# A windowed-attention and gated-feed-forward block: later chunks' normalized rows turned through DRAM and 32x32 blocks

## The chip, the core and the metric

The kernel runs on one core of one Trainium2 chip. The metric is device time in microseconds, median of the runs. One core has TensorE (matrix products; its weight loads are shown as a stream of their own), VectorE, ScalarE, GpSimd and SyncE (SP), which issues most DMA transfers. Each engine works off its own list of instructions in order; semaphores hold an instruction back until what it reads is there. A DMA issue waits on its queue too, so what stands behind a waiting issue waits with it.

## The reference

The block takes 2048 rows of 640 features, all inputs bf16. It normalizes the rows, computes attention over a sliding window of 256 rows with 32 heads of 20, and a gated feed-forward with 1536 hidden features, and adds both to the input.

```python
def reference(A_x, A_wqkv, A_wo, B_x, B_w_gate, B_w_up, B_w_down):
    x = A_x
    xn = _layernorm(x, axis=-1)          # (x - mean) / sqrt(var + 1e-5)
    return x + _A_ref(xn, A_wqkv, A_wo) + _B_ref(xn, B_w_gate, B_w_up, B_w_down)

def _A_ref(x, wqkv, wo):
    B, S, D = x.shape
    H = 32; Dh = D // H; W = 256
    qkv = (x @ wqkv).reshape(B, S, 3, H, Dh).transpose(2, 0, 3, 1, 4)
    q, k, v = qkv[0], qkv[1], qkv[2]
    scores = jnp.einsum("bhqd,bhkd->bhqk", q, k) * (Dh ** -0.5)
    idx = jnp.arange(S)
    mask = (idx[:, None] - idx[None, :] >= 0) & (idx[:, None] - idx[None, :] < W)
    p = _softmax(jnp.where(mask[None, None], scores, -1e9), axis=-1)
    o = jnp.einsum("bhqk,bhkd->bhqd", p, v)
    return o.transpose(0, 2, 1, 3).reshape(B, S, D) @ wo

def _B_ref(x, w_gate, w_up, w_down):
    g = jnp.einsum("bsd,df->bsf", x, w_gate)
    u = jnp.einsum("bsd,df->bsf", x, w_up)
    return jnp.einsum("bsf,fd->bsd", _sigmoid(g) * u, w_down)
```

## The kernel before

**Chunks.** The rows go in four chunks of 512 (c = 0 to 3), each of four blocks of 128 rows (s). A chunk's rows lie in xc, rows on partitions. They are normalized into xn, and turned into xnT, features on partitions: 5 groups (d) of 128 features by 512 rows. All projections read xnT, one group after the other as five accumulating matmuls.

**Stages of a chunk.** g_qk makes Q and K in five blocks each; VectorE (Q) and ScalarE (K) copy each block out of PSUM to st, and SP sends it to a scratch in DRAM and reads it back spread over heads (spread). g_v makes V: per row block two halves, copied out by VectorE (first half) and ScalarE. g_gu makes the twelve blocks (f) of the feed-forward: a gate product pg with a tanh on ScalarE, an up product pu, and h from both on VectorE. scores, and pv later, run the attention in groups of heads: products into ps, an exponential on ScalarE into pT, masks on pT by GpSimd (the affine selects), products into acc; finish_group and scale_group transpose and scale acc on VectorE into oc. g_out makes the output: per row block the down projection over the twelve h (down), the wo product (add_wo), the addition of x (add_x) and the store.

**The order.** It is written out by hand, as a list of parts (fill) that the attention steps pull work from: an attention step's products go to TensorE, and then as much of the other work as its credit allows. All g_... functions are generators that emit a piece of work and yield its cost on TensorE. mix(a, b, first, every, rest) emits a piece of b behind every `every`-th piece of a from piece `first` on, and with rest what is left of b at the end. Pieces of cost 0 (VectorE's, DMA issues) change nothing in TensorE's order. Each engine's list follows the order of emission; the accumulators come from four PSUM banks in turn (ps_d), so a product waits until the bank's reader from four products ago is done.

**The norms.** Chunk 0's are made in the prologue and turned by TensorE (transpose_rows). For chunks 1 to 3, g_norms emits per row block the statistics (ln_block, two BN_STATS and an aggregation; behind the fourth, GpSimd makes rstds of all four), then `gap` empty pieces, then per block the norm (norm_block, L272), and a piece later that block's transfer from xn to xnT, a transposing DMA on SP (turn_block, L283). xn has four buffers of 128 x 640. Chunk 3's transfers are emitted apart (g_turns). Where they stand:

- norms1 (chunk 1): behind the feed-forward pieces of chunk 0 (gu0a from its fifth piece, gu0b);
- norms2: in out0, chunk 0's output part;
- norms3: statistics behind gu1b's pieces (chunk 1's feed-forward blocks 7 to 11), norms and transfers in out1, with the gap of 6.

**SP's list around chunk 1.** load_rest (L187) issues the last four quarters of the feed-forward weights, then spread of chunk 0's other head groups; then come chunk 1's four transfers, chunk 2's rows (load_x), wo by way of a DRAM tile (turn_wo), wd, and the zero rows of the second scratch. The last quarter, wu[1] from FS // 2 on, holds up-weights for the blocks f = 9 to 11. SP has eight completion semaphores in turn, so an issue also waits for the landing of the one eight before it.

**Others that the change touches.** make_edge (L238) fills the tile edge for masks of later chunks, on GpSimd, after chunk 0's g_qk; new_rows (L447) loads x's rows for the last addition into the three rows buffers and, for the last block, into an xn buffer.

Of the kernel before, what the change touches and what calls it, by code (L numbers as in the profile page):

```python
# [9 lines left out]
P = 128  # L10
S = 2048
D = 640
# [3 lines left out]
DC = D // P  # L16
FC = F // P
CW = 512
NCH = S // CW
SBC = CW // P  # L20
# [6 lines left out]
FS = 768  # L27
# [4 lines left out]
MULT = mybir.AluOpType.mult  # L32
SUB = mybir.AluOpType.subtract
# [60 lines left out]
def kernel(  # L94
# [85 lines left out]
    def load_gu(t, w, k, lo=0, hi=FS):  # L180
        nc.sync.dma_start(out=t[k][:, :, lo:hi],
                          in_=w.rearrange("(c p) f -> p c f", p=P)[:, :, k * FS + lo:k * FS + hi])
# [7 lines left out]
    def load_rest():  # L190
        load_gu(wg, B_w_gate, 1, 0, FS // 2)
        load_gu(wu, B_w_up, 1, 0, FS // 2)
        load_gu(wg, B_w_gate, 1, FS // 2)
        load_gu(wu, B_w_up, 1, FS // 2)
        spread("q", 0, 4, NG)
        spread("k", 0, 4, NG)

# [38 lines left out]
    edge = const.tile([P, HG, 2 * U], BF16, name="edge")  # L236

    def make_edge():  # L238
        nc.gpsimd.memset(edge, BIG)
        for k, base, sign in ((0, -1, -1), (1, 0, 1)):  # L240
            for a in range(2):
                view = edge[a * U:(a + 1) * U, :, k * U:(k + 1) * U]
                nc.gpsimd.affine_select(out=view, in_=view, pattern=[[0, HG], [sign, U]],
                                        compare_op=GE, fill=0.0, base=base, channel_multiplier=-sign)

    xnT = {}
    xns = {}

    def ln_half(c, s, a, stats=None):
        if a == 0:  # L250
# [17 lines left out]
        return rstds  # L268

    def norm_block(c, s, mv, rstd):  # L270
        xn = lnp.tile([P, D], BF16, name="xn")
        nc.vector.tensor_scalar(out=xn, in0=xc[c][:, s, :], scalar1=mv[:, 0:1],  # L272
                                scalar2=rstd[:, 0:1], op0=SUB, op1=MULT)
        xns[c, s] = xn

    def transpose_rows(s, copy, lo=0, hi=DC):
        pt = ps_h.tile([P, DC, P], BF16, name="pt", tag="h")
        for d in range(lo, hi):
            nc.tensor.transpose(pt[:, d, :], xns[0, s][:, d * P:(d + 1) * P], ident)  # L279
        copy(out=xnT[0][:, lo:hi, s * P:(s + 1) * P], in_=pt[:, lo:hi, :])  # L280

    def turn_block(c, s):
        nc.sync.dma_start(out=xnT[c][:, :, s * P:(s + 1) * P], in_=xns.pop((c, s)), transpose=True)  # L283

    def new_xnT(c):
        xnT[c] = xtp.tile([P, DC, CW], BF16, name="xnT")
# [53 lines left out]

    MM = 216

    def g_norms(c, turn, gap=3):


        new_xnT(c)
        mvs = lnp.tile([P, SBC, nc.vector.BN_AGGR_DIM], FP32, name="mvs", bufs=1)
        for s in range(SBC):
            ln_block(c, s, mvs[:, s, :])
            if s == SBC - 1:  # L350
                rstds = rstd_blocks(mvs)
            yield 0
        for _ in range(gap):
            yield 0
        for s in range(SBC):
            norm_block(c, s, mvs[:, s, :], rstds[:, s:s + 1])
            yield 0
            if turn:
                turn_block(c, s)

    def g_turns(c):
        for s in range(SBC):
            turn_block(c, s)
            yield 0

    def g_qk(c):
        for w in "qk":
            for m in range(DC):
                proj_block(w, c, m)
                if c == 0 and w == "q" and m == 1:  # L370
                    load_x(1)
                if c == 0 and w == "q" and m == 3:
                    load_gu(wu, B_w_up, 0, FS // 2)
                if c == 1 and w == "q" and m == 3:
                    load_wo()
                if c and w == "k" and m == DC - 1:
                    spread("q", c, 0, GH)
                yield 5 * MM
        if c == 0:
            spread("q", c, 0, 2)  # L380
            spread("k", c, 0, 2)
            spread("q", c, 2, 4)
            spread("k", c, 2, 4)
# [60 lines left out]
            out=rows[:, cut[0]:cut[1]], in0=y[:, 0:cut[1] - cut[0]], scalar=0.5,  # L444
            in1=rows[:, cut[0]:cut[1]], op0=MULT, op1=ADD)

    def new_rows(c, s, name="rows", bufs=3, queue=nc.sync):  # L447
        rows = lnp.tile([P, D], BF16, name=name, bufs=bufs)
        queue.dma_start(out=rows, in_=xr[:, c * SBC + s, :])
        return rows  # L450

# [11 lines left out]
    def g_out(c, between, ahead=()):  # L463
        nxt = new_rows(c, 0)
        for s in range(SBC):
            rows = nxt
            if s == 0:
                yield from ahead
            if s + 1 < SBC:
                nxt = new_rows(c, s + 1)  # L470
            ys = [ps_d.tile([P, CW], FP32, name=f"y{i}", tag="d") for i in range(2)]
            for y, cut in zip(ys, HALVES):
                yield from down(c, s, y, cut)
            if s == 0:
                yield from between
            outp(c, s, ys, rows)
            yield 10 * 136
# [117 lines left out]
    def mix(a, b, first, every=1, rest=True):  # L595

        for k, cost in enumerate(a):
            yield cost
            if k >= first and (k - first) % every == 0:
                yield next(b, 0)  # L600
        if rest:
            yield from b
# [9 lines left out]
        norm_block(0, s, mv, r)  # L612

    def mean_act(s):
        xn = lnp.tile([P, D], BF16, name="xn")
        neg = lnp.tile([P, 1], FP32, name="neg")
        nc.scalar.activation(out=xn, in_=xc[0][:, s, :], func=IDENTITY, scale=-1.0 / D, accum_out=neg)  # L617
        return xn, neg
# [7 lines left out]
    def norm_act(s, xn, neg, r):  # L626
        nc.vector.reciprocal(r, r)
        nc.vector.tensor_scalar(out=xn, in0=xc[0][:, s, :], scalar1=neg[:, 0:1],  # L628
                                scalar2=r[:, 0:1], op0=ADD, op1=MULT)
        xns[0, s] = xn  # L630

    new_xnT(0)
    for s in range(SBC):
        new_v(0, s)
    act, dve = nc.scalar.copy, nc.vector.tensor_copy
# [33 lines left out]
    nc.scalar.activation(out=scr, in_=neghalf[:, 0:1], func=EXP)  # L669
    banks.close()  # L670
    ps_s = banks.enter_context(tc.tile_pool(name="ps_s", bufs=1, space=bass.MemoryType.PSUM))
    for _ in g_qk(0):
        pass
    load_rest()
    make_edge()

    fill = Fill()
    GU = 10 * MM
# [4 lines left out]
        load(*args)  # L683
        yield 0

    norms1 = g_norms(1, True)
    norms2 = g_norms(2, True)
    norms3 = g_norms(3, False, 6)
    fill.add("gu0a", mix(g_gu(0, 0, 4), norms1, 4, 1, False), 4 * GU)
    fill.add("gu0b", mix(g_gu(0, 4, 12), norms1, 0), 8 * GU)  # L690
    fill.add("x2", later(load_x, 2), 0)
    fill.add("wo_i", later(turn_wo), 0)
    fill.add("wd", later(load_wd), 0)
    fill.add("pads", later(clear_next), 0)
    fill.add("qk1", g_qk(1), 50 * MM)
    fill.add("v1", mix(g_v(1), g_gu(1, 0, 2), 1, 2), 40 * 136 + 2 * GU)
    fill.add("out0", mix(g_out(0, g_gu(1, 2, 3)), norms2, 1, 1), OUT + GU)
    fill.add("x3", later(load_x, 3), 0)
    fill.add("qk2", g_qk(2), 50 * MM)
    fill.add("v2", mix(g_v(2), g_gu(1, 3, 7), 0, 1), 40 * 136 + 4 * GU)  # L700
    fill.add("gu1b", mix(g_gu(1, 7, 12), norms3, 0, 1, False), 5 * GU)
    fill.add("out1", mix(g_out(1, g_gu(2, 0, 1)), itertools.chain(norms3, g_turns(3)), 1, 2), OUT + GU)
    fill.add("qk3", g_qk(3), 50 * MM)
    fill.add("v3", mix(g_v(3), g_gu(2, 1, 5), 0, 1), 40 * 136 + 4 * GU)
    fill.add("gu2", g_gu(2, 5, 12), 7 * GU)
# [41 lines left out]
        for _ in gen:  # L747
            pass

    homes = [("rows", 3)] * (SBC - 1) + [("xn", 4)]  # L750
    rows = [new_rows(c, s, *home, queue=nc.scalar) for s, home in enumerate(homes)]
    banks.close()
    ps_y = pool("ps_y", 4, space=bass.MemoryType.PSUM)
    ys = {}
# [52 lines left out]
```

## Time and profile before

| what | value |
|---|---|
| median of 3 runs | 309.23 us (308.93 to 309.33) |
| span of the profiled execution | 307.5 us |
| TensorE busy in it | 299.6 us |
| VectorE busy | 170.7 us |
| ScalarE busy | 198.4 us |
| GpSimd busy | 169.3 us |
| chunk 1's transposing transfers issued | 39.32 to 44.59 us |
| chunk 2's | 93.28 to 101.35 us |
| chunk 3's | 162.58 to 173.89 us |

The span goes from the first to the last instruction of the program; the runs' time has launch and end around it, 1.7 us. In an order of time each row shows start, duration, engine, line, operation, tiles, count, and in brackets the idle time before it with what ended it. Where two instructions of one engine overlap by some ten ns, the later has begun before the earlier has drained; the distance of their starts is what one of them costs the engine. A row of a group has busy time and the mean of one in ns. A row of a stretch has its limits, its length, each engine's busy time and count in the order TensorE, its weight loads, VectorE, ScalarE, GpSimd, and then TensorE's granted clock, the DMA engines' share and GB/s.

### The profile page before, as it was taken

How to read it: one execution, taken by the hardware profiler on the slowest of the kernel's cores; microseconds unless marked ns; L12 is line 12 of the kernel's file. 1: busy time of each engine (PE TensorE's matmuls, PEld its weight loads, DVE VectorE, ACT ScalarE, POOL GpSimd, SP SyncE). 2: the span in 40 equal slices, each digit the busy share in tenths (PEclk: the TensorE clock that was granted, in tenths of full speed). 3: DMA queues.
4: the chain of work that ended last, by engine and by line, in shares of the span. 5: the costliest groups of instructions: out<-in, count | busy, mean ns of one | idle time of the engine just before them, and what ended most of it. 6: DMA issues, size and time to landing. Idle time of an engine off the chain costs nothing.

```text
span 307.5 us, 9944 instructions
## 1 busy us (share of the span) xinstructions
PE 299.6 (97%) x4276; PEld 167.5 (54%) x4311; DVE 170.7 (56%) x339; ACT 198.4 (65%) x197; POOL 169.3 (55%) x308
## 2 busy tenths in 40 slices
PE   7999999999999999999999999999999999999995
PEld 3654444555657654554457654554546664444774
DVE  5633666639698364487946164392824536363523
ACT  6933877698855649888674547878585547687000
POOL 6000686787874828576683729467372937566000
PEclk9999999999999999999999999999999999999999
DMA  7997976986407352820002712730000200000202
GB/s 215 366 344 236 324 158 214 337 238 209 154 2 139 58 179 68 272 83 2 3 3 67 129 58 87 250 122 0 5 0 2 87 26 21 2 2 7 83 21 67
DMA packets 40460, 35.68 MB, mean 116 GB/s; under 512 B 10560, under 2 KB 39872, under 8 KB 40384
## 3 DMA queue, kind: packets, MB, share of 16 engines
q1 hardware_dynamic: 39552, 34.27, 37.3%
q10 hardware_dynamic: 864, 0.77, 0.9%
q8 instruction: 34, 0.56, 0.8%
q14 instruction: 10, 0.08, 0.1%
HBM read 23.63 MB, written 10.26 MB: 110 GB/s over the span
## 4 chain that ended last, share of the span: by engine, by line
PE 96%; issue 1%; DMA 1%; DVE 1%; ACT 0%; SPq 0%
PE y L432 18%; PE pu L418 17%; PE pg L411 17%; PE pqk L297 14%; PE ps L487 9%; PE pv L326 7%; PE y L439 7%; PE acc L520 6%; DMA xc<-in_A_x_dram 1%; PE pt L279 0%; ACT xn L617 0%; DVE xn L272 0%; DVE xn L628 0%; SPq L156 0%; DVE stats L252 0%
## 5 line engine op out<-in xcount | busy, mean ns | idle before, releaser
L504 POOL TENSOR_SCALAR_AFFINE_SELECT pT<-pT 64x512 bf16<-64x512 bf16 (+1 forms) x256 | 157.7, 616 | 108.1 <-ACT pT L493 95.6
L493 ACT ACTIVATE pT<-ps 128x2048 bf16<-128x2048 f32 (+1 forms) x76 | 141.0, 1855 | 59.6 <-PE ps L487 54.6
L422 DVE SCALAR_TENSOR_TENSOR h<-th,pu 128x512 bf16<-128x512 f32 x48 | 32.8, 684 | 52.6 <-PE pu L418 46.1
L418 PE MATMUL pu<-xnT,wu 128*128 128x512 bf16 x228 | 59.0, 380 | 0.7 <-issue 0.2
L411 PE MATMUL pg<-xnT,wg 128*128 128x512 bf16 x226 | 58.5, 380 | 0.9 <-issue 0.3
L432 PE MATMUL y<-wd,h 128*128 128x320 bf16 (+2 forms) x396 | 56.7, 295 | 0.0
L432 PEld LDWEIGHTS <-h 128*128 128x128 bf16 x396 | 36.7, 98 | 15.8 <-issue 2.0
L414 ACT ACTIVATE th<-pg 128x512 f32<-128x512 f32 x48 | 28.6, 595 | 15.5 <-PE pg L411 15.4
L411 PEld LDWEIGHTS <-wg 128*128 128x128 bf16 x240 | 22.2, 98 | 25.8 <-issue 1.8
L418 PEld LDWEIGHTS <-wu 128*128 128x128 bf16 x240 | 22.0, 98 | 25.5 <-issue 2.0
L487 PE MATMUL ps<-qT,kT 20*64 20x320 bf16 (+4 forms) x1440 | 32.1, 260 | 0.0
L532 DVE STREAM_TRANSPOSE t<-acc 128x512 f32<-128x512 f32 x32 | 21.1, 697 | 19.7 <-PE acc L520 19.7
L487 PEld LDWEIGHTS <-kT 20*64 20x64 bf16 x1440 | 15.4, 103 | 24.9 <-issue 21.8
L443 DVE SCALAR_TENSOR_TENSOR rows<-y,rows 128x320 bf16<-128x320 f32 x30 | 14.4, 488 | 25.5 <-PE y L439 25.3
L544 DVE TENSOR_TENSOR on<-t,rec 128x320 bf16<-128x320 f32 (+4 forms) x48 | 27.8, 580 | 1.1
L326 PE MATMUL pv<-wv,xnT 128*128 128x320 bf16 x160 | 25.7, 300 | 0.0
L439 PE MATMUL y<-wo,oc 128*128 128x320 bf16 (+2 forms) x165 | 24.2, 295 | 0.0
L297 PE MATMUL pqk<-xnT,wk 128*128 128x512 bf16 x97 | 23.1, 381 | 0.2
L297 PE MATMUL pqk<-xnT,wq 128*128 128x512 bf16 x94 | 22.8, 381 | 0.4 <-issue 0.2
L335 DVE CAST v<-pv 64x320 bf16<-64x320 f32 x29 | 14.1, 486 | 12.5 <-PE pv L326 12.3
L520 PE MATMUL acc<-pT,v 64*32 64x320 bf16 (+4 forms) x1440 | 19.7, 253 | 0.0
L520 PEld LDWEIGHTS <-v 64*32 64x32 bf16 x1440 | 16.2, 91 | 5.8 <-ACT pT L493 1.7
(50 smaller groups left out, 178.7 us busy)
## 6 DMA issues: line engine op xcount, KB each, us to landing
qT<-sq SPq DMA_DIRECT2D x16, 256.0 KB
kT<-sk SPq DMA_DIRECT2D x16, 256.0 KB
sq<-st SPq DMA_DIRECT2D x20, 128.0 KB
sk<-st SPq DMA_DIRECT2D x20, 128.0 KB
out_dram<-rows SPq DMA_DIRECT2D x15, 160.0 KB
wg<-in_B_w_gate_dram SPq DMA_DIRECT2D x4, 480.0 KB
wu<-in_B_w_up_dram SPq DMA_DIRECT2D x4, 480.0 KB
xc<-in_A_x_dram SPq DMA_DIRECT2D x3, 640.0 KB
```

Source lines behind the costliest of these rows:

```text
L297: nc.tensor.matmul(ps, lhsT=wt[:, m, :], rhs=xnT[c][:, d, :], start=(d == 0), stop=(d == DC - 1))
L326: nc.tensor.matmul(ps[:, 0:HALF], lhsT=xnT[c][:, d, s * P:(s + 1) * P], rhs=wqkv[2][:, d, hf * HALF:(hf + 1) * HALF], start=(d == 0), stop ...
L411: nc.tensor.matmul(pg, lhsT=part(wg, d, f), rhs=xnT[c][:, d, :], start=(d == 0), stop=(d == DC - 1))
L414: nc.scalar.activation(out=th, in_=pg, func=TANH, scale=0.5)
L418: nc.tensor.matmul(pu, lhsT=part(wu, d, f), rhs=xnT[c][:, d, :], start=(d == 0), stop=(d == DC - 1))
L422: nc.vector.scalar_tensor_tensor(out=h, in0=th, scalar=1.0, in1=pu, op0=ADD, op1=MULT)
L432: nc.tensor.matmul(y[:, 0:cut[1] - cut[0]], lhsT=ht[c, f][:, s * P:(s + 1) * P], rhs=wd[:, f, cut[0]:cut[1]], start=(f == 0), stop=False)
L439: nc.tensor.matmul(y[:, 0:cut[1] - cut[0]], lhsT=oc[c, m][:, s * P:(s + 1) * P], rhs=wo[:, m, cut[0]:cut[1]], start=False, stop=(m == DC - 1))
L487: nc.tensor.matmul(ps[a * U:(a + 1) * U, i, col * U:(col + n) * U], lhsT=qk["k", kc, o // GH][32 * i:32 * i + DH, o % GH + a, kb * U:(kb + ...
L493: nc.scalar.activation(out=pt[:, :, 0:width], in_=ps[:, :, 0:width], func=EXP, scale=SCALE)
L504: nc.gpsimd.affine_select(out=view, in_=view, pattern=[[0, HG], [0, n], [sign, U]], compare_op=GE, fill=0.0, base=base, channel_multiplier ...
L520: nc.tensor.matmul(acc[32 * i:32 * i + 32, q * U:(q + n) * U], lhsT=vt[kb][a * U:(a + 1) * U, u, h * VW:h * VW + 32], rhs=pt[a * U:(a + 1) ...
```

## The change

For chunks 1 to 3 the transposing DMA goes. norm_grouped writes a normalized row block with its features in another order: feature 128 d + 32 b + i goes to column 160 b + 32 d + i, so that the five pieces of 32 features that end on one group b of 32 partitions lie together (160 values, 320 B). put_rows sends the block as it is to a DRAM tile xs (one for odd, one for even chunks). regroup reads that tile back into the same xn, which is now one tile of 128 x 4 x 640, in four DMAs, one for each b: partition 32 b + j gets from row 32 t + j (t = 0 to 15) the 160 values of group b. turn then makes one group d of xnT with one VectorE transpose of 32x32 blocks, 128 x 512, out of runs of 32 values that lie 160 apart; five turns make a chunk. Chunk 3's rows are put in two transfers of two blocks (pair = 2), the others' in four.

In the lists: `lag` empty pieces stand between regroup and the turns. norms1 starts behind gu0a's second piece, with gap 3 and lag 6; chunk 2's statistics move behind the last pieces of qk1 and its norms come at once in out0 (gap 0, lag 8); chunk 3's gap is 2, so that its norms are emitted in gu1b, with regroup and turns in out1 (lag 6). The load of wu[1] from FS // 2 on is issued behind chunk 1's regroup. make_edge is emitted ahead of chunk 0's g_qk, with its memset on VectorE. The last block's rows go into the xn tile.

```diff
--- before.py
+++ after.py
@@ -191,7 +191,6 @@
         load_gu(wg, B_w_gate, 1, 0, FS // 2)
         load_gu(wu, B_w_up, 1, 0, FS // 2)
         load_gu(wg, B_w_gate, 1, FS // 2)
-        load_gu(wu, B_w_up, 1, FS // 2)
         spread("q", 0, 4, NG)
         spread("k", 0, 4, NG)
 
@@ -236,7 +235,7 @@
     edge = const.tile([P, HG, 2 * U], BF16, name="edge")
 
     def make_edge():
-        nc.gpsimd.memset(edge, BIG)
+        nc.vector.memset(edge, BIG)
         for k, base, sign in ((0, -1, -1), (1, 0, 1)):
             for a in range(2):
                 view = edge[a * U:(a + 1) * U, :, k * U:(k + 1) * U]
@@ -246,6 +245,9 @@
     xnT = {}
     xns = {}
 
+    def new_xn(c):
+        xns[c] = lnp.tile([P, SBC, D], BF16, name="xn", bufs=1)
+
     def ln_half(c, s, a, stats=None):
         if a == 0:
             stats = lnp.tile([P, 2, nc.vector.BN_STATS_DIM], FP32, name="stats")
@@ -268,19 +270,36 @@
         return rstds
 
     def norm_block(c, s, mv, rstd):
-        xn = lnp.tile([P, D], BF16, name="xn")
-        nc.vector.tensor_scalar(out=xn, in0=xc[c][:, s, :], scalar1=mv[:, 0:1],
+        nc.vector.tensor_scalar(out=xns[c][:, s, :], in0=xc[c][:, s, :], scalar1=mv[:, 0:1],
                                 scalar2=rstd[:, 0:1], op0=SUB, op1=MULT)
-        xns[c, s] = xn
 
     def transpose_rows(s, copy, lo=0, hi=DC):
         pt = ps_h.tile([P, DC, P], BF16, name="pt", tag="h")
         for d in range(lo, hi):
-            nc.tensor.transpose(pt[:, d, :], xns[0, s][:, d * P:(d + 1) * P], ident)
+            nc.tensor.transpose(pt[:, d, :], xns[0][:, s, d * P:(d + 1) * P], ident)
         copy(out=xnT[0][:, lo:hi, s * P:(s + 1) * P], in_=pt[:, lo:hi, :])
 
-    def turn_block(c, s):
-        nc.sync.dma_start(out=xnT[c][:, :, s * P:(s + 1) * P], in_=xns.pop((c, s)), transpose=True)
+    xs = [tc.dram_tile([CW, D], BF16, name=f"xs{k}") for k in range(2)]
+
+    def norm_grouped(c, s, mv, rstd):
+        xn = xns[c][:, s, :]
+        nc.vector.tensor_scalar(out=xn.rearrange("p (b d i) -> p d b i", b=4, i=32),
+                                in0=xc[c][:, s, :].rearrange("p (d b i) -> p d b i", b=4, i=32),
+                                scalar1=mv[:, 0:1], scalar2=rstd[:, 0:1], op0=SUB, op1=MULT)
+
+    def put_rows(c, s, n):
+        nc.sync.dma_start(out=xs[c % 2][s * P:(s + n) * P, :].rearrange("(n p) f -> p n f", p=P),
+                          in_=xns[c][:, s:s + n, :])
+
+    def regroup(c):
+
+        rows = xs[c % 2].rearrange("(t j) (b f) -> b j t f", j=32, b=4)
+        for b in range(4):
+            nc.sync.dma_start(out=xns[c][32 * b:32 * b + 32].rearrange("j s (a f) -> j (s a) f", a=4), in_=rows[b])
+
+    def turn(c, d):
+        nc.vector.transpose(out=xnT[c][:, d, :].rearrange("p (t j) -> p t j", j=32),
+                            in_=xns[c].rearrange("p s (a f) -> p (s a) f", a=4)[:, :, 32 * d:32 * d + 32])
 
     def new_xnT(c):
         xnT[c] = xtp.tile([P, DC, CW], BF16, name="xnT")
@@ -340,10 +359,7 @@
 
     MM = 216
 
-    def g_norms(c, turn, gap=3):
-
-
-        new_xnT(c)
+    def g_norms(c, gap, lag, pair=1):
         mvs = lnp.tile([P, SBC, nc.vector.BN_AGGR_DIM], FP32, name="mvs", bufs=1)
         for s in range(SBC):
             ln_block(c, s, mvs[:, s, :])
@@ -352,15 +368,20 @@
             yield 0
         for _ in range(gap):
             yield 0
+        new_xn(c)
         for s in range(SBC):
-            norm_block(c, s, mvs[:, s, :], rstds[:, s:s + 1])
+            norm_grouped(c, s, mvs[:, s, :], rstds[:, s:s + 1])
+            if s % pair == pair - 1:
+                put_rows(c, s + 1 - pair, pair)
             yield 0
-            if turn:
-                turn_block(c, s)
-
-    def g_turns(c):
-        for s in range(SBC):
-            turn_block(c, s)
+        regroup(c)
+        if c == 1:
+            load_gu(wu, B_w_up, 1, FS // 2)
+        for _ in range(lag):
+            yield 0
+        new_xnT(c)
+        for d in range(DC):
+            turn(c, d)
             yield 0
 
     def g_qk(c):
@@ -444,8 +465,9 @@
             out=rows[:, cut[0]:cut[1]], in0=y[:, 0:cut[1] - cut[0]], scalar=0.5,
             in1=rows[:, cut[0]:cut[1]], op0=MULT, op1=ADD)
 
-    def new_rows(c, s, name="rows", bufs=3, queue=nc.sync):
-        rows = lnp.tile([P, D], BF16, name=name, bufs=bufs)
+    def new_rows(c, s, rows=None, queue=nc.sync):
+        if rows is None:
+            rows = lnp.tile([P, D], BF16, name="rows", bufs=3)
         queue.dma_start(out=rows, in_=xr[:, c * SBC + s, :])
         return rows
 
@@ -612,7 +634,7 @@
         norm_block(0, s, mv, r)
 
     def mean_act(s):
-        xn = lnp.tile([P, D], BF16, name="xn")
+        xn = xns[0][:, s, :]
         neg = lnp.tile([P, 1], FP32, name="neg")
         nc.scalar.activation(out=xn, in_=xc[0][:, s, :], func=IDENTITY, scale=-1.0 / D, accum_out=neg)
         return xn, neg
@@ -627,9 +649,9 @@
         nc.vector.reciprocal(r, r)
         nc.vector.tensor_scalar(out=xn, in0=xc[0][:, s, :], scalar1=neg[:, 0:1],
                                 scalar2=r[:, 0:1], op0=ADD, op1=MULT)
-        xns[0, s] = xn
 
     new_xnT(0)
+    new_xn(0)
     for s in range(SBC):
         new_v(0, s)
     act, dve = nc.scalar.copy, nc.vector.tensor_copy
@@ -669,10 +691,10 @@
     nc.scalar.activation(out=scr, in_=neghalf[:, 0:1], func=EXP)
     banks.close()
     ps_s = banks.enter_context(tc.tile_pool(name="ps_s", bufs=1, space=bass.MemoryType.PSUM))
+    make_edge()
     for _ in g_qk(0):
         pass
     load_rest()
-    make_edge()
 
     fill = Fill()
     GU = 10 * MM
@@ -683,23 +705,23 @@
         load(*args)
         yield 0
 
-    norms1 = g_norms(1, True)
-    norms2 = g_norms(2, True)
-    norms3 = g_norms(3, False, 6)
-    fill.add("gu0a", mix(g_gu(0, 0, 4), norms1, 4, 1, False), 4 * GU)
+    norms1 = g_norms(1, 3, 6)
+    norms2 = g_norms(2, 0, 8)
+    norms3 = g_norms(3, 2, 6, 2)
+    fill.add("gu0a", mix(g_gu(0, 0, 4), norms1, 1, 1, False), 4 * GU)
     fill.add("gu0b", mix(g_gu(0, 4, 12), norms1, 0), 8 * GU)
     fill.add("x2", later(load_x, 2), 0)
     fill.add("wo_i", later(turn_wo), 0)
     fill.add("wd", later(load_wd), 0)
     fill.add("pads", later(clear_next), 0)
-    fill.add("qk1", g_qk(1), 50 * MM)
+    fill.add("qk1", mix(g_qk(1), norms2, 6, 1, False), 50 * MM)
     fill.add("v1", mix(g_v(1), g_gu(1, 0, 2), 1, 2), 40 * 136 + 2 * GU)
     fill.add("out0", mix(g_out(0, g_gu(1, 2, 3)), norms2, 1, 1), OUT + GU)
     fill.add("x3", later(load_x, 3), 0)
     fill.add("qk2", g_qk(2), 50 * MM)
     fill.add("v2", mix(g_v(2), g_gu(1, 3, 7), 0, 1), 40 * 136 + 4 * GU)
     fill.add("gu1b", mix(g_gu(1, 7, 12), norms3, 0, 1, False), 5 * GU)
-    fill.add("out1", mix(g_out(1, g_gu(2, 0, 1)), itertools.chain(norms3, g_turns(3)), 1, 2), OUT + GU)
+    fill.add("out1", mix(g_out(1, g_gu(2, 0, 1)), norms3, 1, 2), OUT + GU)
     fill.add("qk3", g_qk(3), 50 * MM)
     fill.add("v3", mix(g_v(3), g_gu(2, 1, 5), 0, 1), 40 * 136 + 4 * GU)
     fill.add("gu2", g_gu(2, 5, 12), 7 * GU)
@@ -747,8 +769,9 @@
         for _ in gen:
             pass
 
-    homes = [("rows", 3)] * (SBC - 1) + [("xn", 4)]
-    rows = [new_rows(c, s, *home, queue=nc.scalar) for s, home in enumerate(homes)]
+    rows = [new_rows(c, s, queue=nc.scalar) for s in range(SBC - 1)]
+    new_xn("last")
+    rows.append(new_rows(c, SBC - 1, xns["last"][:, 0, :], nc.scalar))
     banks.close()
     ps_y = pool("ps_y", 4, space=bass.MemoryType.PSUM)
     ys = {}
```

## The prediction

> **What bounds the kernel now.** I read the engines' shares first, then the chain of waits, then the table of stretches, and last the order of time on VectorE and TensorE around each place where the change moves work.
>
> ```profile
> PE 299.6 (97%) x4276; PEld 167.5 (54%) x4311; DVE 170.7 (56%) x339; ACT 198.4 (65%) x197; POOL 169.3 (55%) x308
> ...
> PE 96%; issue 1%; DMA 1%; DVE 1%; ACT 0%; SPq 0%
> ```
>
> TensorE is busy for 97% and the chain runs on it for 96%. The table of stretches says how much could be won at all:
>
> ```profile
> 13.30:303.00 289.70, 287.44 (x4192) 160.38 (x4226) 161.90 (x316) 188.08 (x173) 164.48 (x286) 1.00 0.37 109
> ```
>
> From 13.3 us, when the projections start, to 303.0 us TensorE idles for 289.70 - 287.44 = 2.26 us, in scraps, at full clock (1.00). The change touches no TensorE instruction: the same instructions stand in the same order in both kernels, and ScalarE's too. So it can give back some of 2.26 us, or put new stalls into a stream that has none. What decides is whether each producer that the change makes later still comes before its reader. Four places are tight.
>
> **Place 1, chunk 1's puts, regroup and the last up-weights (38 to 56 us).**
>
> ```profile
> 30.09 1.31 SPq L181 DMA_DIRECT2D wu<-in_B_w_up_dram  x1
> ...
> 39.32 5.27 SPq L283 DMA_TRANSPOSE xnT<-xn  x4
> 44.64 0.70 SPq L140 DMA_DIRECT2D xc<-in_A_x_dram  x1
> ...
> 92.65 0.43 SPq L449 DMA_DIRECT2D rows<-in_A_x_dram  x1
> ```
>
> ```profile
> 48.27 1.25 PE L418 MATMUL pu<-xnT,wu 128*128 128x512 bf16 x5
> ```
>
> The last quarter of the up-weights is first read at 48.27 us. Today its load is issued at 30.09 us and, by the completion counts of its semaphore in the trace, landed at 38.3 us: 10 us to spare. In the changed order it stands on SP's queue behind four puts and four regroup loads, and the first regroup load waits until all puts have landed. Step by step: chunk 1's statistics now start after the first h, not the second, and its norms run after h 3 to 5, so that the fourth norm follows the h that starts at 38.24 us and ends near 39.4; its put is issued at 39.5 and lands 1.8 us later (the store issued at 92.26 us landed at 94.06): 41.3. Four regroup issues of 0.5 us follow, the first at 41.4. The 160 KB load issued at 92.65 landed at 94.92, 2.27 us later. A regroup load has 512 packets of 320 B, 32 for each DMA engine; the DMA records show 18 ns for a packet of 256 B, 32 for 640 B and 55 for 1280 B, so about 20 ns, 0.65 us a load. The one load here that also fills only 32 partitions at a time (wo from wo_i) took 84 ns for 1280 B instead of the usual 57, which would make it 0.96. The first lands near 44, the fourth at 45.9 to 47.0, and the 480 KB weights 1.5 us behind (that is the distance at which such loads landed, 33.8, 35.3, 36.8, 38.3): 47.4 to 48.5, against 48.27. **Stall 0 to 0.3 us; I take 0.2.**
>
> [...]
>
> Behind the waiting regroup on SP stand also chunk 2's rows (landed at 49.7 today, read by the statistics near 64.6 after the change: 15 us of cover) and the wo and wd transfers, which go out at nearly today's times because the queue no longer holds four transposes (5.27 us of issue). The reads of xnT: VectorE's queue has the first turn behind the scaling that ends at 50.5, then h, two turns, h, two turns.
>
> ```profile
> L548 DVE STREAM_TRANSPOSE oc<-on 128x512 bf16<-128x512 bf16 x20 | 14.2, 712 | 0.7
> ...
> L272 DVE TENSOR_SCALAR xn<-xc,mvs,rstds 128x640 bf16<-128x640 bf16 x12 | 6.9, 602 | 0.2 <-POOL rstds L267 0.2
> ```
>
> A turn is the same operation as the 712 ns row (0.65 from start to start), with the input in runs of 32. So the fifth ends at 50.5 + 5 x 0.65 + 2 x 0.68 = 55.1; its reader, the fifth matmul of the projection that starts at 54.59, comes at 55.46. **Nothing**, with 0.3 us to spare; how slow a strided turn can be is not in the trace. The cheap bound is the row itself; the dear one is twice the row, 1.3 us, since records of one operation spread that far here (norms 0.41 to 0.81 us): that is a rival too.
>
> **Place 2, chunk 2's statistics, moved from the first output part into qk1 (62 to 77 us).** Three blocks (0.99 us each, 87.81 to 88.80) fall into the idle 4.83 us before the transposes of acc; the fourth falls behind them.
>
> ```profile
> 69.41 1.31 DVE L532 STREAM_TRANSPOSE t<-acc 128x512 f32<-128x512 f32 x2 [4.83 <-PE acc L520]
> 70.64 0.95 DVE L335 CAST v<-pv 64x320 bf16<-64x320 f32 x2
> ...
> 74.35 0.99 DVE L335 CAST v<-pv 64x320 bf16<-64x320 f32 x2
> ```
>
> VectorE works without a gap from 69.41 to 77, so everything after 70.64 comes 1.0 us later. The copy of v that ends at 75.34 would end at 76.34, and the next V projection into that PSUM bank loads its weights at 76.11. **Stall 0.3 us** with the wait (0 to 0.7, since the multiplications in between take 0.42 to 1.00 us beside GpSimd). GpSimd gets 1.3 us (rstds, 0.23 and 1.05) ahead of the masks of two steps; the later step's masks end at 81.5 instead of 80.2, and the product that reads them runs at 81.46 plus the stall: taken as nothing. The first output part loses 4 us of statistics and gets 3.3 us of turns behind the scaling that ends at 101; they end near 105, before 107.38. Nothing.
>
> **Place 3, chunk 3's norms, moved from the second output part to the end of gu1b (152 to 155 us).** This is the largest term.
>
> ```profile
> 151.79 0.71 DVE L548 STREAM_TRANSPOSE oc<-on 128x512 bf16<-128x512 bf16 x1
> 152.43 1.46 DVE L422 SCALAR_TENSOR_TENSOR h<-th,pu 128x512 bf16<-128x512 f32 x2
> 153.80 1.21 DVE L272 TENSOR_SCALAR xn<-xc,mvs,rstds 128x640 bf16<-128x640 bf16 x2
> ```
>
> ```profile
> 151.70 1.24 PE L418 MATMUL pu<-xnT,wu 128*128 128x512 bf16 x5
> 152.87 0.42 PE L487 MATMUL ps<-qT,kT 20*64 20x320 bf16 x16
> 153.23 2.62 PE L432 MATMUL y<-wd,h 128*128 128x320 bf16 x18
> ```
>
> VectorE is behind here already: h 10 and h 11 wait until 152.43 for the scaling. The down projection starts at 153.23 and loads h 11 as its twelfth weights, at 154.60. The new order is norm, h 10, norm, norm, h 11, norm. Two h take 1.37 us, three norms 3 x 0.56 (the pair in the row started 0.42 apart and took 1.21): h 11 ends at 152.43 + 1.37 + 1.68 = 155.5. **Stall 0.9 us.** With all three as fast as the fastest record (0.36 to the next start, at 38.85) 0.3, as slow as the slowest (0.79) 1.6. Fewer, larger puts (two of 320 KB) have the whole of 156 to 168 us as cover.
>
> **Place 4, chunk 3's last turn.** It stands behind the last row addition (178.07, 0.49 us), ends near 179.2, and its reader is the fifth matmul of the projection that starts at 178.32, at 179.24. **Stall 0.1 us** (0 to 0.6 with slow turns).
>
> The edge memset on VectorE fits into an idle 0.66 us before 14.18, and TensorE has banks ahead of it there: nothing, 0.7 us (GpSimd's price) without that cover. Prologue and tail are as before.
>
> **The sum.** 0.2 + 0.3 + 0.9 + 0.1 = 1.5 us on the profiled 307.5 us: 309.0. The runs' median lies 1.7 us over that span, which the change leaves alone: 309.23 + 1.5 = **310.7 us**. The parts' ends give 0.3 us (309.5) and 0.3 + 0.7 + 1.6 + 0.6 = 3.2 us (312.4).
>
> **The rivals.**
> - Slow regroup (0.15): the 320 B packets cost twice as much, and the weights land 2.6 us later, at 50.0 to 51.1; the up projection stalls 2.3 us instead of 0.2: 312.8. For it: no packet of this size is in the trace, and 32 partitions at a time were slow. Against it: 18 ns for 256 B.
> - Slow turns (0.06): at 1.3 us, chunk 1's fifth ends at 58.4, a stall of 2.9 us, which covers place 1's 0.2, and place 4 gives 0.6: with places 2 and 3, 309.2 + 2.9 + 0.6 + 1.2 = 313.9. For it: strided input. Against it: the operation's time hardly differs between PSUM fp32 and SBUF bf16 (697 and 712 ns).
> - All hidden (0.13): the norms run at their fastest and the copies between GpSimd's masks too; about 0.3 us: 309.5, no change.
> - Faster (0.04): one mechanism would be that the stretch of the transposes (39 to 47 and 93 to 103 us, 1.2 to 2.2 us of SP for each) holds TensorE back in its scraps of idle time; with half of the 2.26 us gone, 308.1. It decides if places 1 to 3 don't stall at all. Against it: the scraps are spread evenly, and no wait of TensorE names an xnT transfer.
>
> **How the numbers follow.** The forecast has 0.62. A measurement of this kernel can tell about 0.2% (0.6 us) from no change. Faster 0.04; same 0.13; slower 0.62 + 0.15 + 0.06 = 0.83. The range goes from 309.5 (all hidden at its price) to 313.0 (slow regroup): about 0.08 lies below and 0.1 above.
>
> **What would show it.** Place 3: in the changed trace TensorE idles some 0.9 us at the twelfth matmul of y after gu1b, released by h. Place 2: the V projection after 76 us waits for the copy. Place 1: the matmul on wu after 48 us waits for a DMA. A turn's row should read about 710 ns, a norm's 0.45 to 0.8 us. I am wrong if h 11 comes in time (norms then ran ahead of their place or far faster), or if TensorE's matmuls themselves run closer together.

## The result, and the profile after

| | before | changed |
|---|---|---|
| median of five executions | 309.23 us (308.93 to 309.33) | 313.71 us (312.41 to 314.14) |
| span of the profiled execution | 307.53 us | 311.58 us |
| its TensorE granted clock | 1.000 | 0.995 |

The ratio is 1.0138, with a 95% interval of 1.0121 to 1.0154: slower by 4.5 us, three times the 1.5 us of the sum. From the page of the changed kernel: the shares of the engines, the row of the granted clock in 40 slices of 7.8 us, and the chain of waits by engine and by line:

```profile
PE 304.5 (98%) x4311; PEld 167.9 (54%) x4311; DVE 178.4 (57%) x355; ACT 198.4 (64%) x197; POOL 167.9 (54%) x307
...
PEclk9999997999999999999999999999999999999999
...
PE 92%; DMA 4%; DVE 1%; SPq 1%; ACT 1%; issue 1%; DVEq 0%
PE y L453 17%; PE pu L439 16%; PE pg L432 16%; PE pqk L316 14%; PE ps L509 8%; PE pv L345 7%; PE y L460 7%; PE acc L542 6%; DMA wu<-in_B_w_up_dram 2%; DMA xs<-xn 1%; DMA xc<-in_A_x_dram 1%; DVE xn L286 1%; SPq L298 1%; DVE h L443 0%; PE pt L279 0%
```

TensorE is "busier" than before (98%), yet the chain runs on it for 92% instead of 96%, and 4% of it is DMA: above all the last up-weights (wu, 2%) and the last put (xs, 1%). The place is the seventh slice, where the clock has a 7. The order of time on TensorE there (start, duration, instruction; in brackets the idle time before it and its releaser):

```profile
47.94 0.37 PE L509 MATMUL ps<-qT,kT 20*64 20x320 bf16 x16
50.75 2.32 PE L439 MATMUL pu<-xnT,wu 128*128 128x512 bf16 x5 [2.45 <-DMA wu<-in_B_w_up_dram]
52.86 1.84 PE L432 MATMUL pg<-xnT,wg 128*128 128x512 bf16 x5
54.54 0.81 PE L439 MATMUL pu<-xnT,wu 128*128 128x512 bf16 x3
```

TensorE idles 2.45 us for the last up-weights. Then five matmuls of 512 columns take 2.32 us, where five took 1.25 in the kernel before: they run at half the clock. The table of stretches (length; busy time of PE, PEld, DVE, ACT, POOL; granted clock; DMA share; GB/s) shows it beside:

```profile
13.30:48.30 35.00, 35.00 (x344) 16.46 (x342) 17.92 (x36) 21.17 (x25) 14.52 (x27) 1.00 0.88 266
48.30:50.70 2.40, 0.01 (x2) 0.00 (x0) 2.33 (x6) 1.68 (x2) 2.14 (x5) 0.99 1.09 322
50.70:54.10 3.40, 3.35 (x8) 1.19 (x9) 1.40 (x3) 0.00 (x0) 2.04 (x4) 0.51 0.40 154
54.10:60.00 5.90, 5.90 (x56) 2.54 (x55) 3.57 (x7) 4.08 (x4) 1.66 (x3) 1.00 0.88 304
```

In the trace the clock is 0.5 from 50.64 to 54.06 us, for 3.41 us. A slow matmul counts as busy, so the share of PE doesn't show that work got slower. (Nor can the two shares be compared this finely: for the same 4311 weight loads, before's trace holds 4276 matmul records and this one 4311.) The second stall that is to be seen is chunk 3's, in the order of time on VectorE and TensorE:

```profile
155.92 0.71 DVE L570 STREAM_TRANSPOSE oc<-on 128x512 bf16<-128x512 bf16 x1
156.56 0.56 DVE L286 TENSOR_SCALAR xn<-xc,mvs,rstds 128x640 bf16<-128x640 bf16 x1
157.04 0.68 DVE L443 SCALAR_TENSOR_TENSOR h<-th,pu 128x512 bf16<-128x512 f32 x1
157.63 1.11 DVE L286 TENSOR_SCALAR xn<-xc,mvs,rstds 128x640 bf16<-128x640 bf16 x2
158.67 0.67 DVE L443 SCALAR_TENSOR_TENSOR h<-th,pu 128x512 bf16<-128x512 f32 x1
159.26 0.60 DVE L286 TENSOR_SCALAR xn<-xc,mvs,rstds 128x640 bf16<-128x640 bf16 x1
```

```profile
157.36 1.67 PE L453 MATMUL y<-wd,h 128*128 128x320 bf16 x11
159.40 1.12 PE L453 MATMUL y<-wd,h 128*128 128x320 bf16 x7 [0.36 <-DVE h L443]
```

Both traces hold the same 4311 weight loads in the same order, so the distance between equal loads says where the time went:

| weight load | before at | changed at | lag | place in between |
|---|---|---|---|---|
| 300th | 44.40 | 44.37 | -0.03 | |
| 500th | 57.03 | 61.12 | 4.09 | 1 (the first weight load on wu 2.5 us late, 1.6 us half clock) |
| 1100th | 94.81 | 98.93 | 4.13 | 2 |
| 2000th | 146.56 | 150.70 | 4.13 | |
| 2500th | 180.96 | 185.63 | 4.68 | 3 and 4 |
| last | 303.66 | 308.34 | 4.68 | |

Behind the last load this execution's end is 0.63 us shorter than before's; a second profile's is 0.09 us shorter, so that is no effect of the change.

### The profile page after: what moved, and what is told of

Same layout as the page of the kernel before. It is cut to its first block, busy times and chain, and to the rows that moved or that the text cites. A ratio compares the mean times of both kernels' runs of the same rounds, so it can differ in the third digit from the quotient of the medians.

```text
span 311.6 us, 10005 instructions
## 1 busy us (share of the span) xinstructions
PE 304.5 (98%) x4311; PEld 167.9 (54%) x4311; DVE 178.4 (57%) x355; ACT 198.4 (64%) x197; POOL 167.9 (54%) x307
## 4 chain that ended last, share of the span: by engine, by line
PE 92%; DMA 4%; DVE 1%; SPq 1%; ACT 1%; issue 1%; DVEq 0%
PE y L453 17%; PE pu L439 16%; PE pg L432 16%; PE pqk L316 14%; PE ps L509 8%; PE pv L345 7%; PE y L460 7%; PE acc L542 6%; DMA wu<-in_B_w_up_dram 2%; DMA xs<-xn 1%; DMA xc<-in_A_x_dram 1%; DVE xn L286 1%; SPq L298 1%; DVE h L443 0%; PE pt L279 0%
## 5 line engine op out<-in xcount | busy, mean ns | idle before, releaser
L439 PE MATMUL pu<-xnT,wu 128*128 128x512 bf16 x240 | 60.9, 385 | 2.4 <-DMA wu<-in_B_w_up_dram 2.4
L432 PE MATMUL pg<-xnT,wg 128*128 128x512 bf16 x240 | 60.4, 383 | 0.0
L566 DVE TENSOR_TENSOR on<-t,rec 128x320 bf16<-128x320 f32 (+4 forms) x48 | 26.4, 549 | 1.1
```

What stands on the lines that cost most here:

```text
L432: nc.tensor.matmul(pg, lhsT=part(wg, d, f), rhs=xnT[c][:, d, :], start=(d == 0), stop=(d == DC - 1))
L439: nc.tensor.matmul(pu, lhsT=part(wu, d, f), rhs=xnT[c][:, d, :], start=(d == 0), stop=(d == DC - 1))
```

## The experiments

Two theories. **Late weights:** putting the last up-weights behind the puts and the regroup on SP's queue is what costs, by a wait and by the clock that falls with it. **Long path:** the way through DRAM and VectorE itself is too long for chunk 1, wherever the weights stand.

Each ratio is to executions of the kernel before beside it. These had a median of 309.13 us beside early_wu, wu_between, mended and late_wu_4 and of 309.07 us beside the others; beside wo_later and wo_later_all a single one read 310.14.

**early_wu:** the load stands where it stood before.

```diff
     def load_rest():
...
+        load_gu(wu, B_w_up, 1, FS // 2)
...
     def g_norms(c, gap, lag, pair=1):
...
         regroup(c)
-        if c == 1:
-            load_gu(wu, B_w_up, 1, FS // 2)
```

> The changed kernel with the last quarter of the up-weights loaded where it was before, ahead of chunk 0's spread; all else as changed. Theory 'late weights': the 2.6 us wait at the up projection after 48 us and the 1.7 us of half clock behind it go; the puts and regroup land some 1.5 us later, which may stall chunk 1's first projection by up to 1 us; with the h of place 3 (0.5) and the copy of place 2 (0.2) the median comes to 309.9 to 310.9 us, granted clock 1.000. Rival 'the turned path is too long': chunk 1's xnT is late as soon as the weights aren't, TensorE waits 3 us or more at the first projection near 55 us, and the time stays above 312 us.

310.93 us (309.43 to 311.91), ratio 1.0043 (1.0021 to 1.0066): by the medians some 60% of the loss is gone, and its profile shows no half clock (a mean of 0.999, a 9 in each of the 40 slices).

**wu_between:** the load stands between the puts and the regroup.

```diff
+        if c == 1:
+            load_gu(wu, B_w_up, 1, FS // 2)
         regroup(c)
-        if c == 1:
-            load_gu(wu, B_w_up, 1, FS // 2)
```

> The changed kernel with that load issued between chunk 1's puts and its regroup, where SP waits anyway. Late weights: they land near 44.5 to 46 us, before 48.3, no wait, no half clock; the regroup lands about 1 us later (50 to 51 us), so the first turn waits a little; 309.8 to 310.8 us. The turned path is too long: 312 us or more, with the wait at the projections near 55 us.

309.75 us (309.45 to 311.23), ratio 1.0011 (0.9989 to 1.0033). Its order of time at place 1 and its wait at place 3:

```profile
48.07 0.37 PE L509 MATMUL ps<-qT,kT 20*64 20x320 bf16 x16
48.37 1.25 PE L439 MATMUL pu<-xnT,wu 128*128 128x512 bf16 x5
49.46 1.24 PE L432 MATMUL pg<-xnT,wg 128*128 128x512 bf16 x5
```

```profile
PEld L453 <- DVE h L443: 0.7, 1, 0.7
```

No pause, five matmuls in 1.25 us again. The weights landed at 44.12 and the four regroup loads still at 45.85 to 48.51, in time for the turns. One issue moved by four places on one queue brings back nearly all of the 4.5 us, so the long path falls for chunk 1; only place 3 is left.

**mended:** wu_between, and the statistics and norms of chunks 2 and 3 in other gaps.

```diff
-    norms2 = g_norms(2, 0, 8)
-    norms3 = g_norms(3, 2, 6, 2)
+    norms2 = g_norms(2, 1, 8)
+    norms3 = g_norms(3, 5, 3, 2)
...
-    fill.add("qk1", mix(g_qk(1), norms2, 6, 1, False), 50 * MM)
+    fill.add("qk1", mix(g_qk(1), norms2, 5, 1, False), 50 * MM)
```

> As wu_between, and chunk 2's statistics one piece earlier (from the sixth piece of qk1, gap 1), and chunk 3's first norm behind the eleventh h (gap 5, lag 3). If places 2 and 3 cost what the changed trace shows (0.1 to 0.3 and 0.5 us), it is 0.5 to 0.8 us faster than wu_between and within 0.5 us of the kernel before: 309.2 to 309.9 us. If these stalls only move to other readers, it is as wu_between.

309.32 us (308.87 to 310.65), ratio 1.0000 (0.9980 to 1.0020); no wait of the down projection on h is left. The new turn is as fast as the old one and no faster: TensorE is the bound in both, busy for 98% of the span here and for 97% in the kernel before. No version beat the kernel before.

**late_wu_4:** the opposite test. The kernel before with only the load moved, behind chunk 1's DMA transposes and four dummy loads of 160 KB (their tiles are loaded again by the real ones). No put, regroup or turn is in it.

```diff
     def load_rest():
...
-        load_gu(wu, B_w_up, 1, FS // 2)
...
     def g_norms(c, turn, gap=3):
...
+        if c == 1:
+            for _ in range(4):
+                new_rows(0, 0)
+            load_gu(wu, B_w_up, 1, FS // 2)
```

> The kernel before, transposing DMA and all, with only the last up-weights issued behind chunk 1's transposes and four loads of 160 KB of rows that nothing reads (they hold the queue for about 1.8 us). No puts, no regroup, no turns. Late weights: TensorE waits 1.5 to 2.5 us at the up projection after 48 us; if a wait of this length also brings the clock to a half for a while, 312 to 313.5 us in all, if not 310.8 to 311.8. Rival, that the half clock belongs to the turns' or the regroup's load and not to the wait: clock 1.000 here whatever the wait.

316.36 us (315.36 to 317.56), ratio 1.0217 (1.0170 to 1.0264): slower than expected, since the fourth dummy waited for the first to leave one of the three buffers (issued at 48.69, the first had landed at 48.67) and the weights came at 53.3 us. Its order of time:

```profile
53.32 2.31 PE L421 MATMUL pu<-xnT,wu 128*128 128x512 bf16 x5 [4.97 <-DMA wu<-in_B_w_up_dram]
55.43 1.61 PE L414 MATMUL pg<-xnT,wg 128*128 128x512 bf16 x5
```

A late weight load alone makes the same picture, with half clock from 52.74 to 56.16 us. What length of pause does that? The same kernel with 0, 2 and 3 dummies:

> The kernel before with one edit: the load of the last up-weights is issued behind chunk 1's four DMA transposes, with no dummy load ahead of it. Nothing of the new turn is in it. Theory (a weight load that lands after need costs its wait, and once TensorE has idled long enough a half-clock spell of 3.41 us worth 1.6 to 1.7 us besides): landing estimated near 47 to 48.5 us against a need of 48.2, so a wait of 0 to 0.5 us, granted clock 1.0 throughout, median 309.1 to 309.7. Rival (the half clock comes with any pause at this place, whatever its length): 3.4 us of 0.5 clock already here, median 310.8 or more.

> The same with two dummy row loads of 160 KB ahead of the weight load (their data is loaded again by the later, real loads). Theory: with four dummies the wait was 5.0 to 5.2 us and the clock fell to 0.5 for 3.41 us; with two the wait is estimated at 1 to 2 us. If the clock stays at 1.0, the time is the wait alone, 310.1 to 311.2; if it falls as in the changed kernel (2.4 to 2.7 us of wait), 311.7 to 312.9. Rival (length plays no part): half clock whatever the wait.

> The same with three dummy row loads ahead of the weight load: a wait estimated at 1.7 to 3 us. Theory: a wait of 2.4 us or more brings the half clock again, and the time is 309.1 plus the wait plus 1.6 to 1.7 us: 312.8 to 313.8; under that length without the half clock 310.8 to 311.5. Rival (the changed kernel's spell came from the lower PE load or the DMA traffic of its new transfers, not from the pause): clock 1.0 and 310.8 to 312.1.

late_wu_0: 310.69 us (310.60 to 312.83), ratio 1.0051 (1.0034 to 1.0068). late_wu_2: 312.28 us (311.18 to 313.08), 1.0099 (1.0072 to 1.0126). late_wu_3: 314.70 us (313.64 to 315.56), 1.0178 (1.0146 to 1.0210). The waits were longer than expected, 2.0, 2.3 and 3.6 us in the profiled executions (late_wu_0's began 1.7 us late and is its longest). late_wu_2's profiled execution is its fastest; another of its four took 312.71 us at a mean clock of 0.993, as low as in the profiled executions that have one spell (0.993 to 0.995). The order of time of late_wu_2, then of late_wu_3:

```profile
50.64 1.25 PE L421 MATMUL pu<-xnT,wu 128*128 128x512 bf16 x5 [2.29 <-DVE on L547]
51.73 1.24 PE L414 MATMUL pg<-xnT,wg 128*128 128x512 bf16 x5
```

```profile
52.23 2.31 PE L421 MATMUL pu<-xnT,wu 128*128 128x512 bf16 x5 [3.60 <-DMA wu<-in_B_w_up_dram]
54.33 2.34 PE L414 MATMUL pg<-xnT,wg 128*128 128x512 bf16 x5
```

(The first is put down to VectorE; that execution's waits name the weights for 2.5 us, on the weight load.) A pause of 2.29 us left the clock alone.

**after_again:** the changed kernel, a second profile.

> The changed kernel once more, for a second profile. Theory: the last up-weights land between 50 and 51.2 us, TensorE waits 2 to 3 us for them, the clock then reads 0.5 for about 3.4 us, and the time is 312.4 to 314.2. Rival (the wait or the clock of the first profile was that execution's alone): weights by 49.5 us or clock 1.0, and the time still above 312.

313.74 us, and the half clock again, though the pause was shorter than late_wu_2's:

```profile
50.59 2.30 PE L439 MATMUL pu<-xnT,wu 128*128 128x512 bf16 x5 [2.16 <-DMA wu<-in_B_w_up_dram]
```

So the length alone does not decide, and the threshold of 2.4 us falls. The changes of clock in each trace lie on a grid of 3.41 us (the changed kernel's stretches of full clock last 44.37 and 259.41 us, 13 and 76 times 3.413; the one of the kernel before lasts 303.79, 89 times) whose phase differs from execution to execution (these two traces' first clock records begin at 6.27 and 4.24 us). Laid over the pauses, with the grid counted on from the trace's first change:

| run | pause, us | idle within one step of the grid, us | clock in the next step |
|---|---|---|---|
| wo_later_all (below) | 48.49 to 49.24 | 0.75 | 1.0 |
| late_wu_0 | 50.08 to 52.05 | 1.08, then 0.89 | 1.0, 1.0 |
| late_wu_2 | 48.35 to 50.64 | 0.47, then 1.82 | 1.0, 1.0 |
| late_wu_3 | 48.62 to 52.23 | 1.93, then 1.68 | 0.5, 0.5 |
| wo_later (below) | 49.75 to 51.99 | 2.10 | 0.5 |
| after_again | 48.44 to 50.59 | 2.15 | 0.5 |
| all_partitions (below) | 48.34 to 50.72 | 2.24 | 0.5 |
| changed kernel | 48.31 to 50.75 | 2.33 | 0.5 |
| long_runs (below) | 48.42 to 51.11 | 2.66 | 0.5 |
| late_wu_4 | 48.35 to 53.32 | 0.98, 3.41, then 0.58 | 1.0, 0.5, 1.0 |

In these ten executions, steps at full clock with 1.82 us or less of idle time were followed by full clock, those with 1.93 us or more by half clock. Behind steps that were themselves at half clock it was otherwise: after 1.68 us (late_wu_3) the next was at half clock too, after 0.58 us (late_wu_4) it was not; each is one case. (Ends of matmuls are modelled, so these figures are good to some tenths. That the idle time within one step decides is a reading of this table; no run tested it by itself.)

**Why the weights were so late.** Is the regroup slow because of its 320 B pieces or because it fills 32 partitions at a time?

```diff
 # long_runs: 5,120 B in one run per partition, still 32 partitions
-        rows = xs[c % 2].rearrange("(t j) (b f) -> b j t f", j=32, b=4)
+        rows = xs[c % 2].rearrange("(b j q) f -> b j (q f)", b=4, j=32)
 # all_partitions: 320 B pieces, 128 partitions
+        rows = xs[c % 2].rearrange("(a p) (b f) -> b p a f", p=P, b=4)
```

> The changed kernel, but each of the four regroup loads of a chunk reads 5,120 B in one run per partition, still into 32 partitions (the same 160 KB a load; the rows and features that land are others than the computation wants). In the changed kernel chunk 1's regroup loads landed 1.2 us apart and chunks 2 and 3's 0.87 to 0.9 us apart. Theory A (the 320 B pieces make the regroup slow): spacing near 0.45 us, all four landed by about 45.5 us, last up-weights by about 48.5, time 309.5 to 311. Theory B (32 destination partitions make it slow): spacing stays at 0.75 to 1.2 us, weights after 49.5, time 312 to 314.

> The changed kernel, but each of the four regroup loads spreads its 512 pieces of 320 B over 128 partitions instead of 32 (the same bytes and piece size; the data lands in other places than the computation wants). Theory A (the 320 B pieces): spacing stays at 0.85 to 1.2 us, time 312 to 314. Theory B (32 destination partitions): spacing 0.65 us or less (20 ns a packet over 16 DMA engines), weights by about 49.5 us, time 309.5 to 312.

long_runs took 314.06 us, at the edge of theory B's 312 to 314; all_partitions 315.18, above the times of both. For the single packet theory B (the 32 partitions) holds: over 128 partitions a 320 B packet took 22.6 ns on average (nine of ten 20 ns or less), into 32 partitions 28 to 29 ns (one in ten 45 ns or more). For a whole load neither cause stands out: chunk 2's loads landed 0.70 us apart over 128 partitions and 0.73 in long runs, instead of 0.87. Chunk 1's, which count here, landed 1.07 and 0.87 us apart, instead of 1.22 and 1.09 in the changed kernel's two profiles. The weights landed at 50.67 us (all_partitions) and 51.06 (long_runs) all the same, so part of the delay was elsewhere. In all_partitions fourteen of the sixteen DMA engines had finished the weights by 48.79, the last two at 49.88 and 50.67. Behind the load and chunk 2's rows stand the eight wo_i transfers, whose packets of 25.6 KB take 0.95 us each (the median of 32 in the changed kernel's first profile).

```diff
 # wo_later; wo_later_all has the edit of all_partitions too
-    fill.add("wo_i", later(turn_wo), 0)
     fill.add("wd", later(load_wd), 0)
+    fill.add("wo_i", later(turn_wo), 0)
```

> The changed kernel with one edit: the eight wo_i transfers, which move 25.6 KB a packet from DRAM to DRAM at 0.97 us a packet, are issued behind the five wd loads instead of ahead of them, so that they no longer follow closely on the last up-weights' load. In the changed kernel's two profiles the last of the sixteen DMA engines finished that load at 50.71 and 50.55 us, up to 0.9 us behind the fifteenth. Theory (the wo_i packets on the same DMA engines hold the last piece back): fifteenth and sixteenth finish within 0.3 us of each other, weights by 50.0, a wait of 1.2 to 1.9 us, and 0.5 us or more less than 313.7. Rival (the weights are late because the puts and the regroup ahead of them are, and the straggler comes from elsewhere): weights at 50.3 to 51.1, the wait 2 us or more, time 312.4 to 314.2.

> The same edit together with the regroup loads spread over 128 destination partitions (320 B pieces; the data lands elsewhere than the computation wants). Spread alone, the pieces took 22.6 ns on average instead of 28 to 29, yet the weights landed at 50.67. Theory (32 partitions cost about 0.17 us a load, and the wo_i packets hid that): weights by 49.3, wait under 1.3 us, clock 1.0 throughout, time under 311.8. Rival: weights still after 50.2, time above 312.4.

wo_later 315.42 us: the pause 2.24 us, the half clock there (this execution began 1.4 us late). The last two DMA engines finished the weights 0.07 us apart, as that theory has it, but at 51.87 and 51.94 us, and in the changed kernel's first profile they were just as close (50.66 and 50.71). By itself the edit brought nothing: the theory falls. wo_later_all 311.33 us, with this order of time:

```profile
49.24 1.25 PE L439 MATMUL pu<-xnT,wu 128*128 128x512 bf16 x5 [0.75 <-DVE rec L562]
50.33 1.24 PE L432 MATMUL pg<-xnT,wg 128*128 128x512 bf16 x5
```

The weights landed at 49.19, the pause shrank to 0.75 us, and the clock stayed; chunk 1's regroup loads landed 0.88 us apart. So it looks as if each cause alone hid the other, but each of these four versions ran once: that is not shown.

**early_wu_again:** where early_wu's slower executions lose their time.

> The changed kernel with the last up-weights' load back at its old place, for a second profile; its first was its fastest execution (309.43 of 309.43 to 311.91). Theory (with the weights early, the turn path of chunk 1 is at its edge, and in the slower executions the first query and key projections of chunk 1 wait for the last turned block): one idle stretch of 0.3 to 2.5 us in 50 to 57 us that ends on a turn or a regroup load, time 309.8 to 311.9. Rival (its extra time lies with chunk 3's norms near 155 us): no idle in 50 to 57 us, and over 0.7 us behind the activation at 155 us.

310.56 us, and its TensorE has no idle stretch of over 0.15 us between 40 and 60 us, so that the turns of chunk 1 came in time, though the last regroup load landed only at 51.09. Its lag grows in scraps instead: 0.3 us between 60.6 and 73.9 us, 0.56 at place 3, 0.3 near 207. The theory falls; the rival named place 3, but gave it more than it has. The three add up to some 1.2 us.

## Why the prediction was wrong

**The frame held, but for the scraps.** No TensorE instruction moved, and the loss came from producers that were late, at places that the prediction had named. The 2.26 us of scraps could not be won, since they are not idle time: before's trace lacks 35 records of 512-column matmuls (4276 for 4311 weight loads) and shows 34 gaps instead, 30 of them of 52 or 53 ns. In the changed kernel's trace, which has all 4311, TensorE is busy for 253.13 of the 253.50 us from 54.1 to 307.6 us, and what is missing is place 3's wait; in late_wu_2's, the kernel before with only a load moved, for all of the 253.00 us from 52 to 305.

**Place 1 is the step that failed**, "Stall 0 to 0.3 us; I take 0.2". Its mechanism was right (the matmul on wu waits for a DMA), its size was not: 4.1 us, of them 2.5 us of wait. The wait first, by the completion counts of the semaphores:

| | forecast | measured | second profile |
|---|---|---|---|
| last put landed | 41.3 | 42.75 | 42.11 |
| first regroup load landed | 44 | 45.79 | 45.24 |
| distance of the next three | 0.65 to 0.96 | 1.22 | 1.09 |
| last up-weights landed | 47.4 to 48.5 | 50.71 | 50.55 |

The chain was 1.45 us late at the last put and, against the late end of the range, 2.4 at the fourth regroup load (49.45 for 47.0) and 2.2 at the weights. The 1.8 us for a put came from a store with a fairly free way: from 92 to 95 us of before the DMA engines are busy for 0.51 of their time, from 34 to 38 us of the changed kernel for 1.10 and from 38 to 41 us for 0.82. Here the puts stood behind the loads of kT from sk, the last of which landed at 41.12; then the four puts came 0.4 us apart. In the first profile it was one engine's doing: fifteen of the sixteen had finished the last put by 41.20, as forecast, the sixteenth at 42.75. In the second profile the fifteen took until 41.77 and the last until 42.11. What held it is not shown. A regroup load was priced by the median packet, and that was right (20 ns); but a load takes the sum of its packets, and at the changed trace's mean of 29 ns 32 packets make 0.93 us, not 0.65 (the range's late end, 0.96, has it). The trace of before could have told: its 256 B packets have a median of 18 ns and a mean of 27. The slow-regroup rival had nearly this stall (2.3 us for 2.5), by double the price of a packet and so 2.6 us more; no run shows that doubling: the median stayed at 20 ns, and the tenth of the packets at 45 ns and more and the queue ahead made the load late, the wo_i packets behind it perhaps.

The other 1.6 us the prediction did not have in any case: the clock. The profile of before could not show it, since nothing there pauses (2.26 us of idle time in 289.70), and its clock is 1.00 all along (one record, from 4.24 to 308.03 us). A sum with the 2.5 us wait in it would still have come out these 1.6 us short.

**Place 2**, forecast 0.3 us: the lag grew by 0.04 us over it. The copy was 0.24 us late at one weight load, as foreseen, and the stream had it back soon after.

**Place 3**, forecast 0.9 us, measured 0.55. The order was exactly the forecast one, norm, h, two norms, h, norm; from the scaling's end to the end of h 11 it took 2.71 us (156.63 to 159.34) instead of 1.37 + 1.68 = 3.05.

**Place 4**, forecast 0.1 us: not to be seen. The turns were as cheap as taken:

```profile
L301 DVE STREAM_TRANSPOSE xnT<-xn 128x512 bf16<-128x512 bf16 x15 | 9.8, 686 | 0.0
L286 DVE TENSOR_SCALAR xn<-xc,mvs,rstds 128x640 bf16<-128x640 bf16 x12 | 6.7, 593 | 0.0
```

686 ns for a turn with strided input against 712 for the row it was priced by; that rival fell. Without place 1's error the sum is 0.6 us, about 309.8, which is what wu_between took.

**What stays open.** In three of the changed kernel's five executions the mean granted clock reads 1.000, and they took 312.41, 313.71 and 314.14 us. The first is about what 2.5 + 0.55 us of waiting without the half clock give (310.6 us of span, 310.7 measured). The other two are as long as those with the half clock, and a reading of 1.000 doesn't prove that they ran without it: wu_between's trace, too, reads 1.000, and it holds no record of the clock at all. No profile here settles it; nor what early_wu's median has over the 0.1 and 1.3 us that its two profiles show.

## What to carry to other kernels

A load that is moved behind others on a queue must be priced with the queue as it is then: what is still landing when it is issued, and what a packet takes there on average, not at the median (here 29 ns, not 20); and its 10 us of earlier slack must be found again somewhere. A pause of TensorE can cost more than its length: of the ten pauses in the table, the two of 0.75 and 1.97 us were followed by full clock, seven of the eight from 2.15 to 4.97 us by half clock or had it begin within them, and in the changed kernel that added 1.6 us to 2.5. So the clock behind a pause is to be read before the pause is priced by its length. And where one issue on a queue can be moved by four places, that is the first thing to try before the new path is blamed (309.75 us in wu_between for 313.71).

## What the runs showed of the hardware

- The clock at the ten pauses, laid over a grid of 3.41 us: seven steps at full clock with 1.93 to 3.41 us of idle time were followed by half clock, those with 1.82 us or less by full clock (wo_later_all, late_wu_0, late_wu_2, the first step of late_wu_4). In the changed kernel the spell lasted 3.41 us (50.64 to 54.06), and five matmuls of 512 columns took 2.32 us in it where five took 1.25 in the kernel before.
- 320 B packets from DRAM into 32 partitions took 20 ns (median) and 28 to 29 (mean) in the changed kernel's two profiles; into 128 partitions 22.6 ns (mean) in all_partitions. Runs of 5,120 B into 32 partitions took 302 ns (median) and 333 (mean) in long_runs. (All for chunk 1.)
- The weights' own packets of 768 B, right behind such a load, took 57 ns on average in the changed kernel (49 in its second profile) and 40 to 42 in the two runs whose load is spread over 128 partitions (all_partitions, wo_later_all).
